# One plan for a whole two-branch kernel, and its FFT convolution cut into five blocks of 128 channels

## The chip, the cores and the metric

The kernel runs on one core of one Trainium2 chip. The metric is the time of one execution on the device in microseconds (us), the median of several runs. TensorE is called PE here (PEld is its loading of weights), VectorE DVE, ScalarE ACT, GpSimd POOL; SP is the engine that only starts DMAs, POOL starts some too.

## The reference, cut to what matters

Two branches share the rows of one input `x` (2048 x 640) and are mixed by a gate. Branch A is attention with 32 heads of 20 channels, over 8 keys at a distance of 2. Branch B is a long convolution of each of the 640 channels with a kernel K that is a sum over 192 complex modes.

```python
g = _sigmoid((x * gate_w).sum(-1, keepdims=True))
a = _A_ref(x, A_wqkv, A_wo)
b = _B_ref(x, B_A_re, B_A_im, B_B_re, B_B_im, B_C_re, B_C_im, B_log_dt, B_Dskip)
return g * a + (1 - g) * b
# in _B_ref:
P = jnp.exp(logdA[:, :, None] * l[None, None, :])
K = jnp.einsum("dn,dnl,dn->dl", Cc, P, dB).real
...
Yf = Uf * Kf[None, :, :, :]
y = irfft(Yf)[:L] + u * Dskip
```

The convolution is done with transforms of 4096 points. The kernel splits 4096 into 32 x 64, so a transform is two steps of matmuls with constants, and the way back is two more.

## The kernel before, in words

**Order of work.** `Plan.add` records tasks: a name, the engines that may run it, a duration for planning, a function that writes the instructions, what it depends on, and buffers taken and given back. The order of the tasks, and whether ACT (`A`) or DVE (`D`) runs a task that may go to either, is a list of numbers computed beforehand (`ORDER`, L48). `Plan.emit` (L137) writes the tasks in that order and chains the instructions of each engine, so each engine, SP and POOL included, works strictly in the list's order. There are two plans. "main" holds the parameters, attention, the generation of K and the convolution's first step. "tail" holds the rest of the convolution (`fft_conv`, L919). It begins after main is closed, with PSUM pools of its own.

**Attention** (branch A): transposes of x (`turn`, L191), projections (`late`, L272, evicted as `lev` into `prj` or `pv` and stored to DRAM), then eight chunks of 256 positions: five products q*k on DVE (L319) summed over heads on PE (`lg`, L325), softmax, five weighings of v on DVE (`pv`, L385, two steps of two channels and one of one), sums over the window on PE (`gat`, L390), evicted as `oT`, the output projection (`wo`, L407), evicted as `ga` and stored to DRAM by SP (`gaS`).

**Generation of K** (`KGen.plan`): ten groups of 64 channels. In each PE makes arguments (`arg`, L711), ACT takes sines (L723) and exponentials (L725), DVE makes three products (`pq`, three instructions, L743 to L745), PE sums over modes with 256 small matmuls (`kmm`, L761), and `fin` (L1147) copies the sum into `E`. After each five groups `KExpand` spreads E to X on DVE (L806), stores it to DRAM (`Kx`, L832 to L835) and loads it back as `kc` (L840) with time on partitions.

**Convolution.** First step (`f1`, `fk` for K, `fu` for the input, L1163): 160 matmuls of 128x256 with a constant, in which real and imaginary parts are columns; 40 evictions of 128x1024 into bufA (K) and big (input). The second step, in tail, runs over eight slices of frequencies: real part and imaginary part of K and of u are made separately, each by two accumulated matmuls with blocks of a constant PHI (L954, 256 matmuls of 320 columns) and evicted by ACT (32 of 128x1280). DVE makes the complex product with four multiplies (`ta`, `tc`, L979) and two additions (L982) a slice. PHI is loaded slice by slice by POOL. The inverse of the second step (L1009) is 320 matmuls on half of the rows, evicted as `cp` (20 of 128x1024) into bufA as C. The last step (`yp`, L1033) is 512 matmuls on 32x32 tiles in six groups; ACT (L1041) and DVE (L1044, L1048) gate, add `gaF`, which is the attention's result read back from DRAM, and SP and POOL store the output (L1057). Loads of gaF (L972) and of the constant psi (L969) are started by SP after POOL copies that pace them.

**PSUM** is cut into pools: main has `ar` (two buffers of two banks, for `turn`, `arg`, the first step), `tb` (two of one), `kb` and `lg` (one each). tail has two buffers of four banks, then four of two, then two of four again.

Of the kernel before, what the change touches and what calls it, by code (L numbers as in the profile page):

```python
# [36 lines left out]
def _attn_consts():  # L37
# [47 lines left out]
), "tail": (  # L85
# [66 lines left out]

class Attn:
# [22 lines left out]
    def window(self, pl, cst, pa):  # L176
# [7 lines left out]
        for n in range(2 * NKT):  # L184
            hf, kt = divmod(n, NKT)
            b = {}

            def turn(_, hf=hf, kt=kt, b=b):
                tx = b["tx"] = pa.tile([128, 2, 512], F32, name="ar")
                for i in range(8):  # L190
                    nc.tensor.matmul(tx[:, i // 4, (i % 4) * 128:(i % 4) * 128 + 128], self.xn[:, 8 * hf + i, kt * 128:(kt + 1) * 128], self.ident[:], start=True, stop=True)  # L191

            def ev(en, hf=hf, kt=kt, b=b):
                evict(nc, en, self.xT[:, hf, kt, :], b["tx"][:].rearrange("p a b -> p (a b)"))
            m = pl.add(f"turn{n}", "P", 0.447, turn, acq=["ar"], eq=1024, rdy=(14.6, 24.0)[hf])
            self.xts.append((m, pl.add(f"tev{n}", "AD", {"A": 0.905, "D": 1.133}, ev, deps=[m], rel=[("ar", m)])))

    def plan_gate(self, pl, cst, pa, g_sb, late):
# [3 lines left out]
        def logit(_):  # L202
            b["gz"] = gz = pa.tile([128, 2, 512], F32, name="ar")
# [47 lines left out]
    def plan_late(self, pl, wk, pvb, ps):  # L251
        nc = self.nc
        self.stored, mms, n, st = {}, [], 0, {}
        prjw = pvb[:, 0:15 * SC].rearrange("p (w e s) -> p w e s", w=3, e=5)
# [3 lines left out]
        for sc in range(NSC):  # L258
            c0 = sc * SC
            for which, dstS, off in ((0, self.qS, 0), (1, self.kS, HALO), (2, self.vS, HALO)):  # L260
                tag, at_ = ("prj", {}) if sc else ("prjw", {})
                evs = []
                for e in range(5):
                    b = {}

                    def mm(_, b=b, which=which, e=e, c0=c0, sc=sc):
                        if sc and "all" not in st:
                            open_(0)
                        b["pp"] = ps.tile([128, 2, 256], F32, name="tb", bufs=2)
# [21 lines left out]
    def plan_core(self, pl, pvb, g_sb, ps):  # L291
# [7 lines left out]
        lastwo = lastlg = lastpr = lastpv = None  # L299
        spreads = []  # L300
        self.npv = 0
        for sc in range(S // C):
# [4 lines left out]
            def load(nm, src, n, w, c0=c0, b=b):  # L307
# [3 lines left out]
                return pl.add(f"{nm}{c0}", "G", 0.87, fn, deps=dep(w), acq=[nm], dma=1.4)  # L311
# [4 lines left out]
            for e in range(5):  # L316
# [4 lines left out]
                def logits(_, e=e, b=b):  # L321
                    if e == 0:
                        b["lg"] = ps.tile([128, W, 64], F32, name="lg")
# [39 lines left out]
            def spread(_, sc=sc, b=b):  # L363
                b["asb"] = wk.tile([128, TB, W * 64], BF16, name="asb")
# [7 lines left out]
            asb = pl.add(f"asb{sc}", "S", 0.55, spread, deps=[st], acq=["asb"], dma=1.6)  # L372
            spreads.append(asb)
            evs = []
            for e in range(0, 5, 2):
                n = min(2, 5 - e)

                def weigh(_, e=e, n=n, b=b):
                    vt = b["vc"]
                    b["pv", e] = pvb[:, 16 * C * (self.npv % 2):16 * C * (self.npv % 2) + 16 * C].rearrange("p (w n c) -> p w n c", w=W, n=2)  # L380
                    self.npv += 1
                    aw = b["asb"][:].rearrange("p b (w t) -> p w b t", t=64)
                    for k in range(n):
                        for_e = bass.AP(vt[:].tensor, vt[:, e + k, :].offset, [list(vt[:].ap[0]), [DIL, W], [64, TB], [1, 64]])
# [52 lines left out]

NST = 192
NTR, NEX = 5, 6
NXT = 10240  # L440
PSTEPS = 26
MAGIC = 12582912.0
U16 = 65536.0 / (2.0 * np.pi)
# [798 lines left out]
```

## Time and profile before

| | us |
|---|---|
| median of 3 runs | 371.55 |
| the runs | 369.85, 373.75, 371.55 |
| the profiled execution, its time | 373.87 |
| its span, first to last instruction | 371.9 |
| busy: PE, DVE, ACT, POOL | 309.6, 308.6, 306.5, 88.0 |
| last product of the generation ends | 250.7 |
| `yp` starts | 346.7 |

How to read the lines below. A line of a group gives the source line, engine, operation, output and inputs by the program's names, partitions x elements, the count, then the busy time of the group in us, the mean duration of one in ns, and the idle time of the engine just before these instructions with what ended it. A line of the timeline gives start and length in us, then the same names, the count of merged instructions, and in brackets the idle time before. A line of a stretch gives its ends and length, and each engine's busy time with the number of instructions; PEclk is the granted clock of PE, 1 being full. A line of a DMA gives what is copied, the issuing queue, the count, the size and the median time from issue to landing. Busy time of an engine counts overlapping instructions once, so sums of durations come out some per cent above it. Durations of matmuls contain their way through the array: the pitch of a row of matmuls is seen only over many.

### The profile page before, as it was taken

How to read it: one execution, taken by the hardware profiler on the slowest of the kernel's cores; microseconds unless marked ns; L12 is line 12 of the kernel's file. 1: busy time of each engine (PE TensorE's matmuls, PEld its weight loads, DVE VectorE, ACT ScalarE, POOL GpSimd, SP SyncE). 2: the span in 40 equal slices, each digit the busy share in tenths (PEclk: the TensorE clock that was granted, in tenths of full speed). 3: DMA queues.
4: the chain of work that ended last, by engine and by line, in shares of the span. 5: the costliest groups of instructions: out<-in, count | busy, mean ns of one | idle time of the engine just before them, and what ended most of it. 6: DMA issues, size and time to landing. Idle time of an engine off the chain costs nothing. (4 is left out here: it accounts for less than half of the span.)

```text
span 371.9 us, 12255 instructions
## 1 busy us (share of the span) xinstructions
PE 309.6 (83%) x5322; PEld 185.4 (50%) x5350; DVE 308.6 (83%) x417; ACT 306.5 (82%) x413; POOL 88.0 (24%) x125
## 2 busy tenths in 40 slices
PE   0269999999999999998879999998998999979440
PEld 0135654435444645545444555566776556548330
DVE  3788997769989999999997999997785299989552
ACT  1498986599879998999999999889778699979441
POOL 8930040025002002321224225520100021210132
PEclk9999999999999999999989999999999899999855
DMA  8982287667433123881649556632640465420154
GB/s 271 370 237 55 70 239 200 198 190 243 151 108 111 39 108 101 236 260 39 178 98 317 138 184 150 197 130 74 214 142 35 104 176 146 115 51 23 38 131 120
DMA packets 38408, 55.66 MB, mean 150 GB/s; under 512 B 23620, under 2 KB 30340, under 8 KB 37844
## 3 DMA queue, kind: packets, MB, share of 16 engines
q0 software_dynamic: 7920, 28.74, 25.6%
q1 hardware_dynamic: 28980, 25.64, 24.1%
q8 instruction: 41, 0.67, 0.7%
q10 hardware_dynamic: 1456, 0.52, 0.5%
q14 instruction: 11, 0.09, 0.1%
HBM read 35.12 MB, written 19.77 MB: 148 GB/s over the span
## 5 line engine op out<-in xcount | busy, mean ns | idle before, releaser
L272 PE MATMUL tb<-bufA 128*128 128x512 bf16 x282 | 72.1, 389 | 5.5 <-ACT bufA L433 2.3
L723 ACT ACTIVATE big<-ar 128x608 bf16<-128x608 int16 x96 | 59.4, 687 | 3.3 <-PE ar L711 2.8
L711 PE MATMUL ar<-Rarg,L 64*128 64x304 bf16 (+1 forms) x480 | 53.0, 278 | 8.2 <-ACT big L723 3.0
L725 ACT ACTIVATE big<-ar 128x864 bf16<-128x864 f32 x60 | 49.6, 919 | 2.7 <-PE ar L711 2.5
L272 PEld LDWEIGHTS <-bufA 128*128 128x128 bf16 x300 | 33.1, 120 | 34.5 <-issue 12.0
L319 DVE TENSOR_TENSOR prod<-qc,kc 128x2048 bf16<-128x2048 bf16 x40 | 47.7, 1220 | 1.8 <-PE lg L325 1.7
L385 DVE TENSOR_TENSOR pv<-vc,asb 128x2048 bf16<-128x2048 bf16 x40 | 47.1, 1220 | 0.8 <-PE tb L390 0.6
L390 PE MATMUL tb<-pv,ident 128*128 128x512 bf16 (+1 forms) x182 | 37.6, 344 | 0.8 <-issue 0.5
L711 PEld LDWEIGHTS <-L 64*128 64x128 bf16 x480 | 21.7, 94 | 31.3 <-issue 26.0
L761 PEld LDWEIGHTS <-pt 128*32 128x32 bf16 (+1 forms) x2560 | 25.0, 92 | 22.9 <-issue 13.3
L761 PE MATMUL kps<-qq,pt 128*32 128x22 bf16 (+1 forms) x2560 | 35.3, 173 | 0.7 <-issue 0.7
L954 PEld LDWEIGHTS <-PHI 128*128 128x128 bf16 x256 | 25.5, 100 | 18.5 <-issue 8.4
L407 PE MATMUL tb<-wo_sb,oT 128*128 128x320 bf16 x160 | 26.8, 300 | 1.0 <-DVE ga L418 1.0
L390 PEld LDWEIGHTS <-ident 128*128 128x128 bf16 x192 | 17.7, 98 | 15.0 <-issue 1.5
L954 PE MATMUL fp<-big,PHI 128*128 128x320 bf16 x128 | 20.8, 307 | 2.6 <-ACT bufA L433 1.1
L433 ACT ACTIVATE sp_u<-fp 128x1280 bf16<-128x1280 f32 x16 | 19.7, 1236 | 3.8 <-PE fp L954 2.7
L954 PE MATMUL fp<-bufA,PHI 128*128 128x320 bf16 x128 | 20.5, 306 | 0.9 <-ACT sp_k L433 0.4
L745 DVE TENSOR_TENSOR qq<-big 128x1408 bf16<-128x1408 bf16 x24 | 21.3, 887 | 0.0
L433 ACT ACTIVATE sp_k<-fp 128x1280 bf16<-128x1280 f32 x16 | 19.7, 1237 | 1.6 <-PE fp L954 1.3
L191 PE MATMUL ar<-ident,xn 128*128 128x128 bf16 x80 | 7.8, 264 | 15.0 <-DMA xn<-in_A_x_dram 13.6
L433 ACT ACTIVATE big<-bp 128x1024 bf16<-128x1024 f32 x18 | 17.8, 1030 | 3.0 <-PE bp L1163 2.4
L433 ACT ACTIVATE prj<-tb 128x512 bf16<-128x512 f32 x27 | 16.1, 598 | 5.0 <-PE tb L272 4.7
(170 smaller groups left out, 573.8 us busy)
## 6 DMA issues: line engine op xcount, KB each, us to landing
asb<-aS SPq DMA_DIRECT2D x8, 512.0 KB, 3.9
PHI<-c_phi POOLq DMA_DIRECT2D x8, 384.0 KB, 4.6
Sprm<-pc SPq DMA_DIRECT2D x12, 240.0 KB, 3.2
L<-Sprm SPq DMA_DIRECT2D x80, 36.0 KB, 2.8
kc<-kS POOLq DMA_DIRECT2D x8, 337.5 KB, 6.0
vc<-vS POOLq DMA_DIRECT2D x8, 337.5 KB, 4.6
xn<-in_A_x_dram SPq DMA_DIRECT2D x4, 640.0 KB, 12.0
qc<-qS POOLq DMA_DIRECT2D x8, 320.0 KB, 5.8
```

Of the source, the lines that this page charges most:

```text
L272: nc.tensor.matmul(ppf, self.wq[:, kt, which * D + e:(which + 1) * D:5], self.xT[:, c0 // 1024, kt, c0 % 1024:c0 % 1024 + SC], start=(kt = ...
L319: nc.vector.tensor_tensor(b[e][:], b["qc"][:, e, :].unsqueeze(1).to_broadcast([128, W, C]), win(b["kc"][:, e, :], 0, W, DIL, C), ALU.mult)
L385: nc.vector.tensor_tensor(b["pv", e][:, :, k, :].rearrange("p w (b t) -> p w b t", t=64), for_e, aw, ALU.mult)
L390: nc.tensor.matmul(b["op", e][:, 0:n, :], ident[:], b["pv", e][:, w, 0:n, :], start=(w == 0), stop=(w == W - 1))
L407: nc.tensor.matmul(apf[:, :320], b["oT"][:, e, i * 128:(i + 1) * 128], wo_sb[:, e, hf * 320:(hf + 1) * 320], start=(e == 0), stop=(e == 4))
L433: nc.scalar.activation(o, i, ACT.Identity)
L711: nc.tensor.matmul(ar[:, g2, a0:a0 + ncol], L[rows, sb, gp, l0:l0 + 128], R[rows, c0:c0 + ncol], start=True, stop=True, tile_position=(64 ...
L723: nc.scalar.activation(dst[:, 2 * gp:2 * gp + 2, sub, :], ar[:].bitcast(I16)[:, :, 0:2 * SW:2], ACT.Sin, scale=SCL)
L725: nc.scalar.activation(dst[:, 2 * gp:2 * gp + 2].rearrange("p g s n -> p g (s n)"), ar[:, :, 0:2 * EW], ACT.Exp)
L745: nc.vector.tensor_tensor(qq[:], trg[:, :, KI:].rearrange("p a (v m) -> p a v m", v=2), exq[:, :, KI:].unsqueeze(2).to_broadcast([128, 32, ...
L761: nc.tensor.matmul(kps[32 * g:32 * g + 32, h, NM * ql:NM * ql + NM], pt[rows, k, v, :], qq[rows, k, v, :], start=(g not in started), stop= ...
L954: nc.tensor.matmul(fp[:, fl, 0:320].rearrange("p (c x) -> p c x", x=32), phis[fb][:, fl, kind, :], B[:, :, 2 * f1 + ri].rearrange("p c q g ...
```

## The change

1. There is one plan, "main"; "tail" is gone. PSUM is one tile of eight banks, from which tasks take fixed places (`Banks`), and some places overlap: a task of the convolution with place `xr` waits for the last tasks of the generation and of the softmax that use these banks (`fin9`, `at7`), one with `yr` for attention's last ones (`ga711`).
2. The generation's ten groups are now taken in five blocks of two (`HC` is 2), in an order of channels given by `PLACE`. After each block comes expansion, store and load of a fifth of K, and that block's convolution. Blocks 0 and 1 can go through while the generation runs. The first step for u of block 2 waits for block 1; the loads of K of blocks 2 to 4, and u's transforms of blocks 3 and 4, wait for the last product (their buffers lie in the generation's ring).
3. The convolution of a block stacks real and imaginary parts on the 128 partitions. The first step makes them by two matmuls with 64-wide outputs on two column halves of the array. The second step is one matmul for each of 32 frequencies instead of two for each part. u's spectrum is copied with its halves swapped by two DMAs from SBUF to SBUF (`sw`, on SP), and DVE multiplies spectrum and swapped spectrum by K's, in place (`ta`, `tb`); the additions of the complex product are made by the inverse's matmuls in PSUM, two for each output, over all 128 rows.
4. Counts: first step 640 matmuls of 64x128 (L957) for 160 of 128x256; second 320 of 128x128 (L974) for 256 of 128x320; inverse 320 of 128x128 over 128 rows (L1032) for 320 over 64; 100 evictions of 128x1024, of which the order gives 79 to ACT and 21 to DVE, for 60 of 1024 (47 and 13) and 32 of 1280 (ACT); 40 multiplies of 128x1024 (L1018, L1020) for the 32 multiplies and 16 additions (some cut in three).
5. Attention weighs one channel at a time and sums it with 40 groups of eight matmuls of 256 columns. PHI is loaded whole, once. gaF is loaded in 16 DMAs (L1202) after the last first step on u and the attention chunks that it needs; psi's halves go into a part of big. The copies that paced these are gone.
6. The last step is the same but for the order of C's channels: its operand and its output are read and written 16 channels at a time.

```diff
@@ ORDER: one list, "main", 1453 numbers; "tail" is removed
+class Banks:
+    PLACES = {"ar": (0, 2, 2), "tb": (4, 1, 2), "kb": (6, 1, 1), "lg": (7, 1, 1), "xr": (6, 2, 1), "yr": (4, 2, 1), "yp": (0, 4, 2)}
...
-HC = NCH // 2
+HC = 2
+NB = NCH // HC
+PLACE = [0, 3, 4, 1, 2]
...
+    def ring(self, name, bl, k):
+        return (("ar",), ("ar",), ("ar", "ar", "xr"), ("ar", "ar", "xr"), ("ar", "ar", "xr") if name == "u" else ("ar", "ar", "xr", "yr"))[bl][k % (4 if bl == 4 and name != "u" else 3 if bl > 1 else 1)]
...
+# first(): four groups n
+                for q in range(8):
+                    src = col(bl, 8 * n + q)
+                    for ri in range(2):
+                        nc.tensor.matmul(b["bp"][64 * ri:64 * ri + 64, q, :], src, self.F1[:, ri, :], start=True, stop=True, skip_group_check=True, tile_position=(0, 64 * ri))
+                evict(nc, en, self.S1[:, n].rearrange("p f (q g) -> p f q g", g=4), b["bp"][:].rearrange("p q (g f) -> p f q g", f=32))
+# second(): four groups k
+                for f in range(8):
+                    nc.tensor.matmul(b["sp"][:, f, :].rearrange("p (n x) -> p n x", n=4), self.Phi[:, 8 * k + f, :], self.S1[:, :, 8 * k + f, :], start=True, stop=True)
+                evict(nc, en, put(k), b["sp"][:].rearrange("p f x -> p x f"))
+# spectra_u(): first, second, then
+            for r in range(2):
+                nc.sync.dma_start(T()[1][64 * r:64 * r + 64], T()[0][64 - 64 * r:128 - 64 * r])
+# rest(): first and second for K, then for k in range(4)
+  ta:   nc.vector.tensor_tensor(T()[0][:, :, fr], T()[0][:, :, fr], slot[k], ALU.mult)   deps=[sk[k], su[k], sw]
+  tb:   nc.vector.tensor_tensor(T()[1][:, :, fr], T()[1][:, :, fr], slot[k], ALU.mult)   deps=[sk[k], sw]
+# inverse, four groups n
+                for q in range(8):
+                    for r in range(2):
+                        t = T()[r].rearrange("p (x g) f -> p x (g f)", g=4)[:, 8 * n + q]
+                        nc.tensor.matmul(b["cp"][:, q, :], t, self.GAB[:, r, :], start=(r == 0), stop=(r == 1))
+                evict(nc, en, self.C[:, PLACE[bl], :, 8 * n:8 * n + 8], b["cp"][:].rearrange("p q x -> p x q"))
...
-                        n = min(2, 5 - e)
-                        nc.tensor.matmul(b["op", e][:, 0:n, :], ident[:], b["pv", e][:, w, 0:n, :], start=(w == 0), stop=(w == W - 1))
+                        nc.tensor.matmul(b["op"][:, k, :], ident[:], b["pv", e][:, w, :], start=(w == 0), stop=(w == W - 1))
```

More of the change, by code (lines that the diff above doesn't have):

```diff
@@ L790, in shift @@
         def shift(_):
-            nc.vector.tensor_tensor(E()[:, 0, :], E()[:, 0, :], self.Dk[:, hf], ALU.add)
+            nc.vector.tensor_tensor(E()[:, 0, :], E()[:, 0, :], self.Dk[:, PLACE[bl]], ALU.add)
         def move(_):
-            nx = X["nx"] = psp.tile([128, 2, 512], F32, name="nxp", tag="ar")
-            for pt, (b0, n) in enumerate(((0, 4), (4, 3))):
-                for k in range(2):
-                    f = FIRST + b0 + k
-                    nc.tensor.matmul(nx[:, pt, 0:n * CH], S12[:, k], E()[:, f:f + n].rearrange("p m c -> p (m c)"), start=(k == 0), stop=(k == 1))
@@ new lines, in second, with mm, ev @@
+    def second(self, pl, pa, name, bl, m1, firsts, put, held, after):
+        nc, es, ms = self.nc, [], []
+        for k in range(4):
+            b, r = {}, self.ring(name, bl, k + 1)
+            def mm(_, k=k, b=b, r=r):
+                b["sp"] = pa.get(r, 128)
+                for f in range(8):
+                    nc.tensor.matmul(b["sp"][:, f, :].rearrange("p (n x) -> p n x", n=4), self.Phi[:, 8 * k + f, :], self.S1[:, :, 8 * k + f, :], start=True, stop=True)
+            def ev(en, k=k, b=b):
+                evict(nc, en, put(k), b["sp"][:].rearrange("p f x -> p x f"))
+            more = held(k)
+            if name == "k":
+                after = ms[-1:] + after
+            elif k:
+                after = ms[:1]
+            m = self.add(pl, f"s{name}{bl}{k}", 0.46, mm, r, bl, deps=firsts + self.ready, after=after, acq=[r] + more, rel=[("S1", m1)], eq=1024)
+            ms.append(m)
+            es.append(pl.add(f"s{name}e{bl}{k}", "AD", {"A": 0.905, "D": 1.13}, ev, deps=[m], rel=[(r, m)]))
+        return ms, es
@@ L1078, in gated_mix_kernel @@
     at = Attn(ctx, tc, x, A_wqkv, A_wo, gate_w, gaS, omS)
-    P, rows, gates, consts = fft_prefetch(ctx, tc, x, omS)
-    F1c = P["F1c"]
-    Bk = P["bufA"][:].rearrange("p (c f q g) -> p c f q g", c=NCH, f=64, q=8)
+    cv = Conv(ctx, tc, x, omS, gaS, out[0])
     c2 = ExitStack()
-    big = ExitStack()
+    big = ctx.enter_context(ExitStack())
     acst = c2.enter_context(tc.tile_pool(name="a2_cst", bufs=1))
@@ L1189, in gated_mix_kernel, with expand, fetch @@
-    fft_conv(tc, P, big, now["big"][:].rearrange("p (c f q g) -> p c f q g", c=NCH, f=64, q=8), gaS, o2)
+    late = at.plan_late(pl, cv.pool, pvb, ps)
+    gate = at.plan_gate(pl, acst, pa, g_sb, late)
+    at.plan_core(pl, pvb, g_sb, ps)
+    xdone = late + [gate[0]]
+    half = {}
+    def expand(bl, f):
+        shift, move, near, own, other, store = kx.expand(bl, lambda: half["E"], now, pa, kg.S12)
+        a = pl.add(f"shift{bl}", "D", 0.1, shift, deps=[f])
+        n1 = pl.add(f"move{bl}", "P", 0.25, move, deps=[f], acq=["ar"], eq=448)
+        n2 = pl.add(f"near{bl}", "AD", {"A": 0.24, "D": 0.30}, near, deps=[n1], after=half.get("x", []), rel=[("ar", n1)])
+        o1 = pl.add(f"own{bl}", "AD", {"A": 1.9, "D": 1.3}, own, deps=[a], acq=["xk"])
+        o2 = half["cp"] = pl.add(f"other{bl}", "AD", {"A": 0.85, "D": 0.45}, other, deps=[o1, n2])
+        half["x"] = [o2]
+        st = [pl.add(f"xst{bl}{e}", e, d, store, deps=[o2], dma=w, rel=[("xk", o1)]) for e, d, w in (("S", 1.25, 1.4), ("G", 0.6, 0.5))]
+        def fetch(e, bl=bl):
+            if (bl, "kc") not in half:
+                o = (None, None, 2048, 0, 20480)[bl]
+                half[bl, "kc"] = now["kk"].tile([128, 64, CH], BF16, name="kc", tag="xkc") if bl < 2 else now["big"][:, o:o + 2048].rearrange("p (t c) -> p t c", c=CH)
+            for g in (0, 1) if e == "S" else (2, 3):
+                kx.load(bl, half[bl, "kc"], g, nc.sync if e == "S" else nc.gpsimd)
+        ld = half[bl, "ld"] = []
+        for e, d in (("S", 1.4), ("G", 1.1)):
+            ld.append(pl.add(f"xld{bl}{e}", e, d, fetch, deps=st, after=list(ld), acq=["xk"] if bl < 2 and e == "S" else [], dma=0.7))
@@ new lines, in fin, with fn @@
+    def fin(c, b, m, m0, fins):
+        bl, cl = c // HC, c % HC
+        def fn(en):
+            if cl == 0:
+                half["E"] = now["kk"].tile([128, NM, CH], BF16, name="E")
+            evict(nc, en, half["E"][:].rearrange("p m (c x) -> p c m x", c=2)[:, :, :, CQ * cl:CQ * cl + CQ],
+                  b["kps"][:, :, 0:CQ * NM].rearrange("p c (q m) -> p c m q", m=NM))
+        f = pl.add(f"fin{c}", "AD", {"A": 0.38, "D": 0.433}, fn, deps=[m] + ([half["cp"]] if cl == 0 and c else []), after=fins[-1:], rel=[("kb", m0)])
+        if cl == HC - 1:
+            expand(bl, f)
+            convolve(bl)
+        return f
@@ new lines, in gated_mix_kernel @@
+    cst = pl.add("consts", "G", 1.1, cv.consts, dma=0.6)
+    phi = pl.add("phi", "G", 0.55, lambda _: nc.gpsimd.dma_start(cv.Phi[:], cv.host["phi"]), after=[cst], dma=3.2)
+    cv.ready = [cst, phi]
+    ub = []
+    for n in range(8):
+        ub.append(pl.add(f"rows{n}", "G", 1.4 if n else 0.7, lambda _, n=n: cv.rows(n), deps=ub[-1:], after=list(at.stored.values()), dma=1.65))
+    gates = [pl.add(f"gates{g}", "G", 0.55, lambda _, g=g: cv.gates(g), after=ub + [gate[1]], dma=0.1) for g in range(4)]
@@ new lines, in gated_mix_kernel, with convolve @@
+    om = pl.add("om32", "D", 0.1, lambda _: nc.vector.tensor_copy(cv.om32[:], cv.omF[:]), deps=gates)
+    cps = []
+    def convolve(bl):
+        cv.pqs = list(kg.pqs)
+        cv.spectra_u(pl, pa, bl, ub, xdone + params)
+        firsts, cp = cv.rest(pl, pa, bl, lambda: half[bl, "kc"], half[bl, "ld"])
+        cps.extend(cp)
+        if bl < 2:
+            for f in firsts:
+                f.rel.append(("xk", half[bl, "ld"][0]))
+    cv.big = lambda: now["big"]
+    kg.plan(pl, pa, pk, params, opened, fin)
@@ new lines, in gated_mix_kernel, with gated @@
+    psi = lambda: now["big"][:, 0:4096].rearrange("p (u r x) -> p u r x", r=2, x=32)
+    psis = [pl.add(f"psi{h}", "S", 0.5, lambda _, h=h: nc.sync.dma_start(psi()[:, 32 * h:32 * h + 32], cv.host["psi"][:, 32 * h:32 * h + 32]), after=kg.pqs, dma=1.6) for h in range(2)]
+    def gated(n):
+        if n == 0:
+            cv.gaF = cv.pool.tile([128, 16, D], BF16, name="gaF", tag="uga")
+        for j in range(4):
+            nc.sync.dma_start(cv.gaF[32 * j + 8 * n:32 * j + 8 * n + 8], cv.gaS[j][8 * n:8 * n + 8])
@@ new lines, in gated_mix_kernel @@
+    gas = []
+    for n in range(4):
+        gas.append(pl.add(f"gaF{n}", "S", 1.6, lambda _, n=n: gated(n), deps=at.gated[2 * n:2 * n + 2], after=cv.lastu + gas[:1], dma=2.0))
+    by = {t.name: t for t in pl.tasks}
+    for t, r, bl in cv.lazy:
+        t.deps += [by[n] for n in {"xr": ("fin9", "at7"), "yr": ("ga711", "lev59")}.get(r, ())]
+        if bl > 2 and t.name[:2] in ("fu", "su"):
+            t.deps.append(kg.pqs[-1])
+    for bl in (2, 3, 4):
+        for t in half[bl, "ld"]:
+            t.deps.append(kg.pqs[-1])
@@ L1192 @@
+    for h in range(2):
+        psis[h].deps += [by[f"fk{3 - h}{n}"] for n in range(4)]
+    cv.last(ctx, pl, pa, cps, gas + [om], psi, psis, c2.close)
+    pl.emit(tc)
 @with_exitstack
```

558 lines of the change are left out of this document (234 added, 324 removed), and 88 rows, old and new, of the table ORDER.

## The prediction, made before the changed kernel was run

> **What bounds the kernel now.** I read the page's first two parts, then the busy time by stretch, then the groups of instructions with shapes kept apart, then single stretches in order of time, then the DMA issues.
>
> ```profile
> PE 309.6 (83%) x5322; PEld 185.4 (50%) x5350; DVE 308.6 (83%) x417; ACT 306.5 (82%) x413; POOL 88.0 (24%) x125
> ```
>
> No engine is the bound of the whole: three stand at 82 to 83%, so the share says nothing until the span is cut where the work changes.
>
> ```profile
> core 0: us, PE busy (x) PEld busy (x) DVE busy (x) ACT busy (x) POOL busy (x), PEclk, DMA share, GB/s
> 0.00:100.00 100.00, 76.95 (x685) 41.27 (x695) 80.20 (x99) 74.95 (x101) 34.73 (x49) 1.00 0.68 206
> 100.00:250.70 150.70, 140.53 (x3193) 78.01 (x3206) 143.83 (x200) 142.28 (x219) 38.03 (x46) 0.99 0.51 148
> 250.70:346.70 96.00, 85.31 (x946) 60.98 (x946) 74.61 (x105) 81.90 (x84) 9.32 (x18) 0.98 0.36 105
> 346.70:371.90 25.20, 6.85 (x512) 5.18 (x512) 9.96 (x16) 7.39 (x10) 5.94 (x12) 0.57 0.40 107
> ```
>
> 250.7 is where DVE ends the last product of the kernel generation, 346.7 where the last step (`yp`) starts. From 100 to 250.7 DVE and ACT are 95.4% and 94.4% busy: full. In the 96 us behind that ACT is 85.3% and DVE 77.7% busy, 81.5% on the mean: here lie 14 us of idle ACT and 21 of idle DVE. Of this stretch, 300 to 340 alone is fuller (DVE 18.93 and 18.45, ACT 18.61 and 17.42 in its two halves of 20 us, 91.8%); the hollow is 250 to 300, attention's end and the passage from one plan to the other.
>
> ```profile
> 290.85 1.24 ACT L433 ACTIVATE sp_u<-fp 128x1280 bf16<-128x1280 f32 x1 [2.30 <-PE fp L954]
> 295.04 0.82 DVE L979 TENSOR_TENSOR ta<-sp_u,sp_k 128x1280 bf16<-128x1280 bf16 x1 [6.92 <-ACT sp_u L433]
> ...
> L433 ACT ACTIVATE sp_u<-fp 128x1280 bf16<-128x1280 f32 x16 | 19.7, 1236 | 3.8 <-PE fp L954 2.7
> L433 ACT ACTIVATE sp_k<-fp 128x1280 bf16<-128x1280 f32 x16 | 19.7, 1237 | 1.6 <-PE fp L954 1.3
> L433 ACT ACTIVATE big<-bp 128x1024 bf16<-128x1024 f32 x18 | 17.8, 1030 | 3.0 <-PE bp L1163 2.4 <-DVE qq L745 0.6
> ...
> L435 DVE CAST bufA<-cp 128x1024 bf16<-128x1024 f32 x8 | 9.3, 1219 | 0.0
> ...
> L979 DVE TENSOR_TENSOR ta<-sp_u,sp_k 128x1280 bf16<-128x1280 bf16 x16 | 12.7, 820 | 8.2 <-ACT sp_u L433 6.9 <-ACT sp_k L433 1.3
> L982 DVE TENSOR_TENSOR Y<-ta,tc 128x1280 bf16<-128x1280 bf16 x14 | 11.6, 826 | 0.5
> L743 DVE TENSOR_TENSOR pt<-big 128x1024 bf16<-128x1024 bf16 x24 | 16.5, 687 | 0.5 <-issue 0.3 <-ACT big L723 0.2
> ```
>
> The first two lines are the seam: ACT 2.30 us and DVE 6.92 us with nothing to do. The others are my prices (busy time of the group, then mean ns of one).
>
> **Work removed and added.** ACT loses 32 evictions of 1280 (19.7 + 19.7), 35 of the first step (17.8 and its sister's 17.0) and 12 of the inverse (a group of 11.4): 85.9. It gains 79 of 1024 at 0.99 (17.8/18): 78.2, so -7.7; nine fewer of 512 from the projections and attention (-5.4) are paid back by three small kinds that come over from DVE (E, X, a transpose: +5.2 with oT). ACT: -7.9. DVE loses ta, tc and Y (40.4 with their small forms) and gains 40 multiplies of 128x1024 at 0.687, 27.5: -12.9. But it makes 21 of the 100 evictions, at 1.22 (25.6), where it made 13 (15.4): +10.2; and five, two and two more of 512 (at 0.69, +6.2, against six fewer of E, 3.1 less) and copies of X in 52 pieces for 22 (small ones have 0.17 to 0.2 each; +4.7), less 1.2 of the rest. DVE: +3.9. Both together -4.0, times 0.96 since neighbours overlap (in the third stretch DVE's rows make 77.6, its busy time 74.6), -3.8: under 2 us an engine. The additions in PSUM that the stacking saves are paid back by where the evictions go.
>
> PE, by pitch: 16 matmuls of 128 columns with a new weight each take 1.06 us and 8 take 0.61, so 0.056 each; the half-array inverse takes 2.20 for 72, 0.031.
>
> ```profile
> 29.36 0.61 PE L191 MATMUL ar<-ident,xn 128*128 128x128 bf16 x8
> ...
> 38.37 1.06 PE L191 MATMUL ar<-ident,xn 128*128 128x128 bf16 x16
> ...
> 334.35 2.20 PE L1009 MATMUL cp<-GAB,Y 64*128 64x128 bf16 x72 [0.26 <-DVE Y L982]
> ...
> 84.48 0.40 PE L325 MATMUL lg<-prod,ind 128*32 128x512 bf16 x4
> ```
>
> Out go 160 at 0.11, 256 at 0.136, 320 at 0.031: 62. In come 640 halves of 64 columns' width and 640 full ones at 0.056 (36). No row has a half-width stationary; four quarter-width ones (last line) take 0.40 where one takes 0.39, so they run side by side: I take 0.031, the sum is 56; the other end is 0.056 with no overlap at all (72), or 0.15 where a load of 94 ns is also bare (132).
>
> [...]
>
> **Where the work lies.** Stretches 2 and 3 hold 218.4 us DVE and 224.2 ACT; less 3.8 they are 438.8. Behind the last product the changed order leaves on ACT 52 evictions (51.0), 13 of attention, a table load and three small (10.5), on DVE 20 evictions (24.4), 32 multiplies (22.0), 9 weighings at 1.19 (10.7) and 4.5 of the rest: 61.5 and 61.6, times 0.96 59.3 each. Before it is 74.6 against 81.9. So the third stretch shrinks and is balanced, and the second takes (438.8 - 118.6)/2 = 160.1 an engine. At the 94.9% it has now, that is 168.7 us, for 150.7. Bounds: 96% (166.8) and 92% (174.0), as swaps and one more round trip hang on the same two PSUM buffers (`ar`).
>
> Third stretch: at the 91.8% of 300 to 340, 64.6 us; ends 94.9% (62.5) and today's 81.5% (72.8). I take 91.8% since attention's last two chunks now fill the gaps, as in 100 to 250.
>
> **Moved and added DMAs.** Five swaps of 2 x 512 KB on SP, five stores and loads of K for two, each smaller; 16 loads of gaF for 8; POOL loses the five late PHI loads and ten pacing copies and stores and loads a fifth of K five times, off the path. Prices: `asb` 512 KB 3.9 us to landing, gaF 5.0, Kx 3.0 to 6.0 (gaS and today's Kx).
>
> ```profile
> asb<-aS SPq DMA_DIRECT2D x8, 512.0 KB, 3.9
> ...
> gaS<-ga SPq DMA_DIRECT2D x8, 320.0 KB, 3.0
> ...
> gaF<-gaS SPq DMA_DIRECT2D x8, 320.0 KB, 5.0
> ...
> Kx<-X SPq DMA_DIRECT2D x2, 640.0 KB, 6.0
> ```
>
> One place stands out. SP runs, in order, gaF0, the store of the fifth block's K, its load (which waits for that store), gaS6, then the swap of block 3. From block 4's first step on u, which releases gaF0: 1.4 + 1.0 issue, 3.0 to 6.0 landing, 0.8 + 0.4 + 0.7 issue, 3.9 to 6.0 landing: 11.2 to 16.3 us. DVE reaches block 3's first multiply after five evictions, one weighing and two multiplies: 8.7. So DVE waits 2.5 to 7.6, ACT with it (two buffers of spectra). PE's own lateness covers a part; I take 4 (ends 0 and 7.6). The end's loads are hidden: behind attention's last eviction gaS7, gaF3 and half of psi take 9.5 to 9.8 us, beside 14 evictions on ACT, 13.7; each us beyond is paid whole.
>
> Blocks 2 to 4 use PSUM banks of the generation and of attention too. The matmul that takes one waits for their last reader (`fin9`, `at7`, `ga711`), and PE's whole queue behind it; the order puts it after them, by one eviction at the closest: none taken, ends 0 and 1.
>
> Last step: 25.2, the same instructions. Its matmuls read 16 elements at a stretch for 160; nothing in the trace reads so short, none to +3 (what PE has of the chain).
>
> **Sum.** 100.0 (first stretch; ACT's work ahead of the first sine is 53.4 by rows for 56.1, no gain taken) + 168.7 + 68.6 (64.6 + 4) + 25.2 = 362.5 span. The profiled execution took 373.87 for 371.9, so 1.97 around it: 364.5. It stands 2.3 above the median 371.55 of the three runs; 362.2, say 362.
>
> **Rivals.**
> Tighter: the second stretch at 96%, the third at 94.9%, no wait on SP: 166.8 + 62.5 for 237.3, 354; with the first sine 3 us earlier 351. For it: conv work gives both engines something at every gap of the generation. Against: 94.9% was never passed for long.
> Sparse chain: the third stretch at today's 81.5% with the 7.6 wait: 72.8 + 7.6 for 68.6, 374; without that wait 366. For it: each block is a chain of four PE steps with an eviction between each. The change then does not do what it says.
> PE the bound (the slower side): stretch 3 asks PE for 320 + 224 full matmuls (30.4), 384 halves (11.7), attention's 80 at 0.11 and 45 at 0.136 (14.9) and about 1.5 of generation: 58.5, as much as DVE and ACT. At 0.056 a half it is 68.3, the stretch 74.4 + 4, time 372: no change. From there on it decides; at 0.08 it is 77.5, 84.4 + 4, 382; at 0.15 (every load bare) 104.4, 113.7 + 4, 411.
> Multiply at one element a cycle: its operands come in runs of 8. If it takes the 1.16 of the f32 tensor_tensor (128x960) for 0.687, DVE has 15 us more in stretch 3 (32 x 0.47): 59.3 + 14.5, 80.4 + 4, 378. Against: Y writes runs of 4 at 0.826 for 1280, no dearer than ta.
>
> **Chances.** Forecast, 354 to 368: 0.54. Tighter: 0.15. Sparse: 0.14. PE: 0.11, of it 0.02 for bare loads. Multiply: 0.06. A measurement of this kernel tells about 1% from no change, 3.7 us. Faster: 0.15, nearly all of 0.54 and a little of the sparse one: 0.69; same 0.14; slower 0.17. The range 347 to 378 leaves out 2 in 10 at most, most of it PE; the likeliest one's own is 354 to 368.
>
> **What would show it.** The last product near 269 and the last step's start near 337; DVE and ACT alike, near 90%, between them; the halves' 16 matmuls in about 0.65 us; a multiply at 0.69; DVE idle 2 to 8 us ahead of block 3's multiplies, by the swap. Wrong it is if PE waits for nothing there while DVE and ACT wait for PE, or if the second stretch falls under 92%.

## The result and the profile after

The changed kernel takes 411.53 us at the median (410.82 to 414.7, four runs), the kernel before 372.51 in the same comparison (369.85 to 373.75): 1.1075 times, 95% interval 1.0987 to 1.1162. It is slower by 39 us; 362 was forecast. The profiled execution took 411.71 for a span of 409.8.

The page's first part of the changed kernel, and the line of its second part for the DMA engines (tenths of busy time in 40 slices) with what they moved:

```profile
PE 326.2 (80%) x6024; PEld 222.3 (54%) x6024; DVE 307.1 (75%) x443; ACT 299.7 (73%) x416; POOL 80.9 (20%) x117
...
DMA  8925773377421628747475447252311579865354
GB/s 276 399 73 162 215 198 114 130 186 228 149 84 35 186 72 287 237 152 195 114 202 146 135 119 211 88 152 99 86 33 22 78 191 94 111 97 75 56 133 130
```

DVE has 1.5 us less work than before and ACT 6.8 (forecast: 3.9 more and 7.9 less); PE has 16.6 more. Slower by 39 us, with less work on the two engines that were full: the time came in idle. Slices 33 to 36 (from 328 us on) read 7, 9, 8, 6 in DMA with 191, 94, 111 and 97 GB/s under them, where slice 2 reads 9 with 399: the transfers were busy and moved little.

Busy time by stretch, cut at the end of the last product (270.2) and at the last step's start (387.7):

```profile
core 0: us, PE busy (x) PEld busy (x) DVE busy (x) ACT busy (x) POOL busy (x), PEclk, DMA share, GB/s
0.00:100.00 100.00, 75.98 (x696) 39.47 (x700) 81.22 (x102) 76.39 (x102) 34.38 (x49) 0.97 0.65 201
100.00:270.20 170.20, 164.76 (x3616) 106.91 (x3615) 158.24 (x250) 156.20 (x235) 38.82 (x53) 1.00 0.53 151
270.20:387.70 117.50, 78.34 (x1218) 70.79 (x1215) 58.16 (x75) 59.75 (x71) 1.74 (x3) 0.85 0.51 88
387.70:409.80 22.10, 7.07 (x504) 5.15 (x504) 9.50 (x16) 7.40 (x10) 5.96 (x12) 0.50 0.44 122
```

The whole loss is in the third stretch: 117.5 us for 68.6, with DVE at 58.2 and ACT at 59.8 us of work (59.3 each forecast), so half of it idle. What ended the idle time there, from the timeline (in brackets the idle time before the instruction and what ended it):

```profile
334.98 0.53 ACT L439 ACTIVATE ga<-banks,g_sb 128x320 bf16<-128x320 f32 x1 [8.90 <-DMA gaS<-ga]
340.44 0.69 DVE L1018 TENSOR_TENSOR big<-big,spare 128x1024 bf16<-128x1024 bf16 x1 [14.62 <-DMA big<-big]
360.50 0.69 DVE L1018 TENSOR_TENSOR big<-big,spare 128x1024 bf16<-128x1024 bf16 x1 [9.01 <-DMA big<-big]
387.75 1.84 PE L1059 MATMUL banks<-bufA,big 32*32 32x160 bf16 x152 [14.35 <-DMA big<-c_psi]
```

Four waits, 46.9 us on three engines (ACT's and the first of DVE's run side by side), and all four are for DMAs that SP issued: a store of `ga` (its buffer is wanted again), the swaps of blocks 3 and 4, and the second half of `psi`. SP's own timeline (start, time in issue, what) shows what they stood behind:

```profile
315.47 1.31 SPq L1202 DMA_DIRECT2D gaF<-gaS  x4
316.88 0.38 SPq L854 DMA_DIRECT2D Kx<-X  x1
317.36 0.65 SPq L855 DMA_DIRECT2D Kx<-X  x1
329.22 1.47 SPq L859 DMA_DIRECT2D big<-Kx  x2
330.80 0.39 SPq L450 DMA_DIRECT2D gaS<-ga  x1
331.29 1.16 SPq L999 DMA_DIRECT2D big<-big  x2
332.50 5.18 SPq L1202 DMA_DIRECT2D gaF<-gaS  x4
337.79 1.11 SPq L999 DMA_DIRECT2D big<-big  x2
339.06 1.76 SPq L1196 DMA_DIRECT2D big<-c_psi  x1
340.87 12.15 SPq L1202 DMA_DIRECT2D gaF<-gaS  x4
356.06 0.38 SPq L450 DMA_DIRECT2D gaS<-ga  x1
373.40 1.28 SPq L1202 DMA_DIRECT2D gaF<-gaS  x4
374.79 0.35 SPq L1196 DMA_DIRECT2D big<-c_psi  x1
```

The order is the one the prediction read; the times are not. The store of K, its two parts issued at 316.88 and 317.36, has landed only when its load starts at 329.22, for 3 to 6 us in the prediction; the swap issued at 337.79 is waited for until 360.5. The chain of waits that ended last has the same transfers (start, time):

```profile
317.36 11.72 DMA Kx<-X
...
337.37 18.63 DMA gaF<-gaS
356.06 17.32 DMA gaS<-ga
...
374.79 12.91 DMA big<-c_psi
```

The last store of `ga` takes 17.3 us, for the 3.0 that a store of `ga` took before. In front of each stands a batch of four `gaF` loads. In the trace's DMA records a `gaF` load is 8 packets of 20480 bytes, one to a partition; the 128 of them took 3.01 us each at the median, 6.8 GB/s, 369 us together. The eight packets of a load run side by side, and the four loads of a batch follow each other (a batch of 10.8 us from 360.7 to 371.5). In the kernel before the packets of `gaF` had 10240 bytes, 32 to a DMA, and took 0.615 us, 16.7 GB/s.

PE's side: 64 half-width matmuls of the first step take 3.88 us, 0.060 each, where the prediction took 0.031.

```profile
302.37 1.06 PE L974 MATMUL banks<-spare,PHI 128*128 128x128 bf16 x16
304.19 3.88 PE L957 MATMUL banks<-F1c,Usb 128*64 128x128 bf16 x64 [0.76 <-ACT spare L456]
```

### The profile page after: what moved, and what is told of

Read it like the earlier page. It is cut to its first block, busy times and chain, and to the rows that moved or that the text cites. A ratio compares the mean times of both kernels' runs of the same rounds, so it can differ in the third digit from the quotient of the medians.

```text
span 409.8 us, 13703 instructions
## 1 busy us (share of the span) xinstructions
PE 326.2 (80%) x6024; PEld 222.3 (54%) x6024; DVE 307.1 (75%) x443; ACT 299.7 (73%) x416; POOL 80.9 (20%) x117
## 4 chain that ended last, share of the span: by engine, by line
PE 45%; ACT 24%; DMA 18%; issue 4%; DVE 4%; SPq 3%; POOL 0%; POOLq 0%; DVEq 0%; ACTq 0%
PE banks L291 10%; PE banks L957 8%; ACT big L750 7%; PE banks L736 6%; PE banks L410 6%; ACT big L748 5%; DMA gaF<-gaS 5%; DMA gaS<-ga 4%; PE banks L430 4%; PE banks L785 4%; DMA big<-c_psi 3%; DMA xn<-in_A_x_dram 3%; DMA Kx<-X 3%; ACT bufA L456 3%; PE banks L974 2%
## 5 line engine op out<-in xcount | busy, mean ns | idle before, releaser
L291 PE MATMUL banks<-bufA 128*128 128x512 bf16 x300 | 75.2, 392 | 5.1 <-DVE bufA L458 3.1
L748 ACT ACTIVATE big<-banks 128x608 bf16<-128x608 int16 x120 | 73.6, 687 | 4.7 <-PE banks L736 3.7
L456 ACT ACTIVATE spare<-banks 128x1024 bf16<-128x1024 f32 x47 | 47.2, 1023 | 29.5 <-PE banks L957 13.9
L736 PE MATMUL banks<-Rarg,L 64*128 64x304 bf16 (+1 forms) x480 | 51.2, 277 | 5.6 <-ACT big L748 3.1
L750 ACT ACTIVATE big<-banks 128x864 bf16<-128x864 f32 x60 | 49.8, 904 | 4.5 <-PE banks L736 4.3
L404 DVE TENSOR_TENSOR pv<-vc,pv 128x2048 bf16<-128x2048 bf16 x40 | 48.2, 1218 | 6.1 <-PE banks L410 4.6
L410 PE MATMUL banks<-pv,ident 128*128 128x256 bf16 x320 | 40.9, 273 | 1.9 <-issue 1.9
L456 ACT ACTIVATE bufA<-banks 128x1024 bf16<-128x1024 f32 x37 | 36.2, 1028 | 7.9 <-PE banks L1032 5.6
L785 PE MATMUL banks<-qq,pt 128*32 128x22 bf16 (+1 forms) x2560 | 36.0, 173 | 0.0
L430 PE MATMUL banks<-wo_sb,oT 128*128 128x320 bf16 x160 | 27.8, 311 | 7.8 <-ACT ga L439 7.8
L974 PE MATMUL banks<-spare,PHI 128*128 128x128 bf16 x320 | 23.1, 221 | 1.5 <-ACT bufA L456 0.5
L1018 DVE TENSOR_TENSOR big<-big,spare 128x1024 bf16<-128x1024 bf16 x8 | 5.5, 688 | 23.7 <-DMA big<-big 23.6
```

Of the source, the lines that this page charges most:

```text
L291: nc.tensor.matmul(ppf, self.wq[:, kt, which * D + e:(which + 1) * D:5], self.xT[:, c0 // 1024, kt, c0 % 1024:c0 % 1024 + SC], start=(kt = ...
L404: nc.vector.tensor_tensor(b["pv", e][:].rearrange("p w (b t) -> p w b t", t=64), for_e, aw, ALU.mult)
L410: nc.tensor.matmul(b["op"][:, k, :], ident[:], b["pv", e][:, w, :], start=(w == 0), stop=(w == W - 1))
L430: nc.tensor.matmul(apf[:, :320], b["oT"][:, e, i * 128:(i + 1) * 128], wo_sb[:, e, hf * 320:(hf + 1) * 320], start=(e == 0), stop=(e == 4))
L456: nc.scalar.activation(o, i, ACT.Identity)
L736: nc.tensor.matmul(ar[:, g2, a0:a0 + ncol], L[rows, sb, gp, l0:l0 + 128], R[rows, c0:c0 + ncol], start=True, stop=True, tile_position=(64 ...
```

## The experiments

Theories at the start. A: a load of 8 rows uses few DMA engines. B: pieces of 20 KB are slow by their length. C: the first step's pitch sets the end. Behind them, as a rival to all, SP's queue by itself. Executions of kernels that are alike up to there differ by up to 7 us in when the last product starts (268.5 to 275.6), so besides the time I give the distance from the last product's start to where the last step's matmuls run on (their first eight may stand earlier): 118.5 us in the changed kernel (269.27 to 387.75), 69.5 forecast (68.6 from that product's end, and 0.9 for the product). Most kernels below were run once. The distance repeats better than the time: it is 78.2 and 78.3 in the two profiled executions of one kernel (e8, e12).

**e1: two steps' rows in one load, at the later one's place.**

```diff
-        for j in range(4):
-            nc.sync.dma_start(cv.gaF[32 * j + 8 * n:32 * j + 8 * n + 8], cv.gaS[j][8 * n:8 * n + 8])
+        for j in range(4 * (n % 2)):
+            nc.sync.dma_start(cv.gaF[32 * j + 8 * n - 8:32 * j + 8 * n + 8], cv.gaS[j][8 * n - 8:8 * n + 8])
```

> The loads of gaF come in 8 DMAs of 16 partitions x 20 KB in place of 16 of 8 partitions x 20 KB: two steps' worth together, at the place of the later step. Changed kernel: 411.5 us. Theory A (few engines: a DMA of 8 rows occupies 8 of the 16 DMA engines, and the trace's 128 packets of 20480 bytes took 3.01 us at the median, 369 us of engine time, 46 us on each of 8 engines but 23 on each of 16): the end comes 15 to 25 us sooner, 387 to 397. Theory B (long pieces: a packet of 20480 bytes is slow by its length, whichever engine takes it): the packets stay near 3 us and the time falls by under 10 us. Theory C (the first step's half-width matmuls, 0.060 us in place of 0.031, set the end): 411, no change.

Measured: 382.42 us, distance 89.3. More than A asked for, and the packets still take 2.72 us each, as B has it. The run changes two things at once, the number of rows and the place on SP; e11 changes the place alone.

**e2: the same loads cut in two, packets of 10 KB.**

```diff
-            nc.sync.dma_start(cv.gaF[32 * j + 8 * n:32 * j + 8 * n + 8], cv.gaS[j][8 * n:8 * n + 8])
+            for v in (0, 8):
+                nc.sync.dma_start(cv.gaF[32 * j + 8 * n:32 * j + 8 * n + 8, v:v + 8], cv.gaS[j][8 * n:8 * n + 8, v:v + 8])
```

> Each load of gaF is cut in two along the positions: 32 DMAs of 8 partitions x 10 KB. The kernel before moved the same bytes in packets of 10240 bytes that took 0.615 us at the median. Theory A (few engines): the same 8 engines carry the same bytes, so 405 to 415. Theory B (long pieces): packets of 10240 bytes near 0.6 to 1.0 us, the batches land in 4 to 6 us in place of 12 to 18, and the time is 370 to 385. Theory C: 411.

Measured: 415.21 us, distance 117.7; packets of 10240 bytes take 1.50 us, again 6.8 GB/s. B falls: the length of a piece does not matter, the rate per packet stays.

**e3: nearly nothing loaded.**

```diff
-            nc.sync.dma_start(cv.gaF[32 * j + 8 * n:32 * j + 8 * n + 8], cv.gaS[j][8 * n:8 * n + 8])
+            nc.sync.dma_start(cv.gaF[32 * j + 8 * n:32 * j + 8 * n + 8, 0:1], cv.gaS[j][8 * n:8 * n + 8, 0:1])
```

> Leaves out 15 of 16 positions of each gaF load (each partition loads its first position's 1280 bytes, and the last step reads that one for all 16), so the output is not the reference's; the same 16 DMAs, the same waits and places on SP's queue. Theories A and B (the gaF transfers are what the end waits for, through the rings behind them): last step starts near 340 in place of 387.8, time 362 to 372. Theory C, or SP's order by itself (a wait on the queue whatever is moved): 400 to 411.

Measured: 382.49 us, distance 84.7. The bytes of `gaF` cost 34 us of the distance and C is not the cause of those; but the time stays above the 362 to 372 of A and B, so 15 us lie elsewhere.

**e4: the loads issued by POOL.** In `gated`, `nc.sync` becomes `nc.gpsimd`, and the task's engine "G".

> The 16 gaF loads as they are, issued from POOL's queue in place of SP's, with the same place in the order. If what costs is that SP's other transfers (Kx, the swaps, the store of ga, psi) stand behind them in the same rings: those land in 3 to 6 us again, and the time falls to 375 to 390. If the DMA engines themselves are what is full (theories A and B): under 10 us gained, 402 to 412. Theory C: 411.

Measured: 412.21 us, distance 116.4, packets of 20480 bytes 2.41 us. From 340 to 360 the DMA share is 0.96 at 126 GB/s. Another queue does not help here: the transfers themselves are still slow. SP's queue has no `gaF` load in it now, and still the swap of block 3, which SP issues from 334.2 on, is there for DVE only at 366.6; POOL's `gaF` loads run from 336.4 to 367.2:

```profile
366.60 0.69 DVE L1018 TENSOR_TENSOR big<-big,spare 128x1024 bf16<-128x1024 bf16 x1 [37.96 <-DMA big<-big]
```

So the slow loads hold up what another queue carries too. The run does not clear the order, though: the first `gaF` load, on POOL from 318.7, now stands ahead of the part of K's store that POOL issues (320.8), and K's load waits for that.

**e5: the same 16 loads of 8 rows, on every fourth partition.**

```diff
-            nc.sync.dma_start(cv.gaF[32 * j + 8 * n:32 * j + 8 * n + 8], cv.gaS[j][8 * n:8 * n + 8])
+            nc.sync.dma_start(cv.gaF[32 * j + n:32 * j + 32:4], cv.gaS[j][8 * n:8 * n + 8])
+    psis = psis[..., [8 * (i % 4) + i // 4 for i in range(32)]]
```

(The gates' load and the output's rows follow the same permutation.)

> The changed kernel with its 16 gaF loads as they are in number, size (8 rows of 20 KB) and order, but row n*8+a of each 32 goes to partition 4a+n in place of 8n+a, so that a load writes every fourth partition of 32 and not 8 neighbours (psi's columns, the gates and the output's rows are permuted to match). Theory A (a DMA of 8 rows occupies 8 engines, and those are the limit): the packets of 20480 bytes keep their 3.0 us and the time its 411. Theory D (8 neighbouring partitions are written through a narrow path, near 54 GB/s a DMA as 8 packets at 6.8 GB/s show, whatever engines carry it): the packets take 0.8 to 1.5 us, the batches land in 4 to 6 us, and the time comes to that without most of the load, 380 to 386.

Measured: 384.25 us, distance 92.1; the packets of 20480 bytes take 1.03 us at the median, 161 us together for 369. Number, size, order and queue of the loads are as in the changed kernel, so A falls, which would have kept 3.0 us, and D stands: where the rows land decides. 26.4 us of the distance are this. The rates: 8 packets at 6.8 GB/s are 54 GB/s into 8 neighbouring partitions, 16 at 7.5 (e1) 120 into 16 neighbours, and 8 at 20.0 160 into the same number of rows spread over 32. The medians of the last two mix packets; the steadiest give 109 (e1, second and fourth load of each batch, 3.0 us a packet) and 215 (e5, third batch, 0.76 us a packet, 26.9 GB/s). What it is that neighbouring partitions share, no run shows; these rates are what was measured.

**e6: on top of e5, weights from neighbouring elements.**

```diff
-        col = lambda bl, s: self.Usb[:, :, 80 * (s // 16) + 16 * PLACE[bl] + s % 16]
+        col = lambda bl, s: self.Usb[:, s, 0:64]
...
-        fs = self.first(pl, pa, "k", bl, lambda bl, s: kc()[:, :, s], ld + self.ready, self.us, ms)
+        fs = self.first(pl, pa, "k", bl, lambda bl, s: kc()[:, 2 * s:2 * s + 2, :], ld + self.ready, self.us, ms)
```

> On top of the permuted rows: the first step's 64-column weights are read from 64 neighbouring elements of x's rows and of the kernel's expansion in place of 64 elements 320 bytes (64 bytes for the expansion) apart, so it transforms other numbers than the reference does; number, size and order of the matmuls stay. Theory C1 (the pitch of 0.060 us per half is the strided weight load, 204 ns against 98 ns for 128 neighbouring columns): the pitch falls to 0.031 to 0.040, PE has 13 to 18 us less work, and the last step starts 6 to 15 us sooner than without this. Theory C2 (two halves of a pair do not overlap one another's load, whatever the stride): the pitch stays 0.056 to 0.062 and the time within 2 us.

Measured: 372.46 us, distance 83.5 for 92.1, and the last product 3.4 us sooner (265.4; 265.8 in e9, while all the kernels with strided weights lie between 268.5 and 275.6). The group of x's weight loads in e5, then in e6 (busy time, mean ns of one; L957 is L958 here, as these kernels have a line more):

```profile
L958 PEld LDWEIGHTS <-Usb 128*64 128x64 bf16 x320 | 19.3, 205 | 1.6 <-issue 1.2
```

```profile
L958 PEld LDWEIGHTS <-Usb 128*64 128x64 bf16 x320 | 10.4, 109 | 3.1 <-issue 2.2
```

The halves that use them, in e5's timeline, then in e6's:

```profile
311.07 3.85 PE L958 MATMUL banks<-F1c,Usb 128*64 128x128 bf16 x64
```

```profile
302.93 1.08 PE L958 MATMUL banks<-F1c,Usb 128*64 128x128 bf16 x32
```

32 halves in 1.08 us, 0.034 each: C1. The halves' pitch comes from the strided weight load: with neighbouring weights it is near the 0.031 that the prediction took. The expansion's weights, 64 bytes apart, load in the same 204 to 205 ns as x's at 320 bytes.

**e7: both halves of psi at the first one's place, on top of e5.** The first task loads both, the second none.

> On top of the permuted rows: both halves of psi are loaded at the place of the first, and none behind the last gaF load. If the last step waits for psi's second half behind the gaF rings: it starts 4 to 14 us sooner than with the permuted rows alone, 368 to 378. If PE's chain sets the start of the last step by itself (as where the gaF loads were left out, 358): within 2 us of the permuted rows.

Measured: 388.51 us, distance 90.9 for 92.1: nothing. The last step's matmuls then wait for an eviction (`bufA`, 1.13 us) and not for `psi`; the chain that ended last runs through a swap, the last store of `ga` and the last `gaF` load. What ended last in the changed kernel was not the only thing that was late.

**e11: on top of e5, the first four loads issued with the next four**, so that nothing of `gaF` waits at the head of SP's queue.

```diff
+        for m in {0: (), 2: (0, 2)}.get(n, (n,)):
+            for j in range(4):
+                nc.sync.dma_start(cv.gaF[32 * j + m:32 * j + 32:4], cv.gaS[j][8 * m:8 * m + 8])
```

> The permuted rows with 16 loads of gaF, the first four of them issued at the place of the next four, so that nothing on SP waits for block 4's first step on u ahead of the fifth block's store of K, the store of ga and the swap of block 3. Measured from the last product to the last step, where single executions compare best: 92.1 us with the permuted rows alone, 78.2 with the pairs. If what the pairs took away is the wait of the first gaF load at the head of SP's queue: 78 to 83 us. If it is the number of DMAs (each waits for the one eight before it on SP, and sixteen loads push the others back by two rounds of eight): 88 to 93 us.

(Eight before: in the trace SP's DMAs of this stretch take eight semaphores in turn, numbers 107, 109 to 114 and 117, and each one waits on its semaphore for the DMA that had it last.)

Measured: 374.38 us, distance 79.5 for 92.1: the first load's wait was worth 12.6 us. SP's timeline in e5, then in e11:

```profile
314.98 2.67 SPq L1203 DMA_DIRECT2D gaF<-gaS  x4
317.76 0.38 SPq L854 DMA_DIRECT2D Kx<-X  x1
...
323.55 1.36 SPq L859 DMA_DIRECT2D big<-Kx  x2
325.02 0.38 SPq L450 DMA_DIRECT2D gaS<-ga  x1
325.51 1.18 SPq L1000 DMA_DIRECT2D big<-big  x2
```

```profile
301.32 0.36 SPq L854 DMA_DIRECT2D Kx<-X  x1
...
304.58 1.47 SPq L859 DMA_DIRECT2D big<-Kx  x2
306.16 0.37 SPq L450 DMA_DIRECT2D gaS<-ga  x1
315.23 1.17 SPq L1000 DMA_DIRECT2D big<-big  x2
317.81 6.67 SPq L1204 DMA_DIRECT2D gaF<-gaS  x8
```

In e5 the store of K starts at 317.8, 2.8 us behind the `gaF` load that waited 21.8 us for block 4's first step on u; without that load in front it starts at 301.3, when its data is ready. The swap of block 3 goes out 10 us sooner, and DVE's wait for it, 11.6 us in e5, is gone.

**e8, e12: pairs of steps on every second partition** (8 loads of 16 rows, the place of e1; psi, gates and output rows follow).

```diff
+        for j in range(4 * (n % 2)):
+            nc.sync.dma_start(cv.gaF[32 * j + n // 2:32 * j + 32:2], cv.gaS[j][8 * n - 8:8 * n + 8])
```

> Two changes to the loads of gaF together: two steps' rows in one DMA at the later step's place (8 DMAs of 16 rows), and row 16n+a on partition 2a+n, so that a DMA writes every second partition of 32. So nothing of gaF waits on SP's queue ahead of the fifth block's store of K and of the store of ga, and half as many DMAs stand between a DMA and the one eight before it on SP. If what is left after the narrow writes is SP's queue (the wait of the first gaF load on block 4's first step, 22 us in which the store of ga and the swap stand behind it, and a queue of eight outstanding DMAs): the last step starts 5 to 12 us sooner than with permuted rows alone (361), the time is 370 to 379. If PE's chain of half-width steps alone sets it (358 where nearly nothing of gaF was loaded): 380 to 384.

> The pairs of gaF loads on every second partition once more, the kernel that computes the whole and was quickest so far, in more rounds. If the narrow writes and SP's queue were all that made the change slower, and the strided weights use up what the change gains: within 1% of the kernel before, 368 to 376. If the change gains besides: under 368.

Measured: e8 377.52 us, four runs from 370.52 to 379.37, too far apart to tell; so it was run again as e12: 373.32 (12 runs) against 373.19 for the kernel before, 0.9993 times, interval 0.9952 to 1.0034. Distance in e12 78.3, against 89.3 in e1, which differs only in the partitions, and 79.5 in e11, which has twice as many loads: the number of DMAs is worth 1.2 us at most. Busy time of e12 in the same stretches:

```profile
0.00:100.00 100.00, 75.09 (x681) 39.37 (x690) 81.29 (x102) 75.76 (x101) 34.63 (x49) 0.98 0.65 201
100.00:269.70 169.70, 164.11 (x3609) 107.16 (x3618) 158.51 (x250) 156.84 (x236) 37.78 (x53) 1.00 0.54 152
269.70:347.00 77.30, 73.13 (x1209) 66.67 (x1207) 58.02 (x75) 59.27 (x71) 1.75 (x3) 1.00 0.52 134
347.00:370.00 23.00, 6.38 (x512) 4.84 (x511) 9.49 (x16) 7.40 (x10) 6.10 (x12) 0.64 0.41 117
```

Now PE is busy 73.1 of 77.3 us in the third stretch, 95%, with DVE and ACT at 75 and 77%: PE is the bound there.

**e9, e10: on top of the pairs, neighbouring weights (as e6), and psi at once (as e7).**

> The pairs of gaF loads on every second partition, and besides the first step's weights from neighbouring elements (other numbers are transformed than in the reference; number and order of the matmuls stay). With the narrow writes, SP's queue and the strided weights all gone, nothing should be left of the difference to the forecast if these three are all of it: 358 to 366, the last step's start 333 to 342. If something else costs (the swaps, the chain of the five blocks): 368 to 374.

> The pairs of gaF loads on every second partition, with both halves of psi loaded at the first one's place. If the last step waits for psi behind the last gaF loads once these are quick: 3 to 6 us below the pairs alone. If it waits for the last gaF loads or for the inverse's evictions: within 2 us.

Measured: e9 362.82 us, distance 72.5. Three removals bring the time to the forecast, in one execution, with other numbers in the first step as in e6. e10 377.75, distance 78.5: `psi` is again worth nothing.

## Why the prediction was wrong

Point by point, in its own order.

- The second stretch: right in time, by luck. The last product starts at 269.27, "near 269", and ends at 270.2 for 268.7, though with 157 us of work an engine for 160 and 92.4% for 94.9%: two misses that cancel.
- The work of the third stretch: right, 58.2 and 59.8 for 59.3. The multiply: 0.69 us as taken (0.683 to 0.688 at the median), so that rival is out.
- The failed step is "The end's loads are hidden", and the price under it, "gaF 5.0". The 5.0 was read from loads of 32 partitions x 10 KB and carried to loads of 8 x 20 KB. With the changed shape a packet has 6.8 GB/s for 16.7, and the slow loads hold up what is in flight beside them: K's store 11.7 us for 3 to 6, a swap 22 for 3.9 to 6.0 (6.1 from its first issue to its last packet in e12, 312.38 to 318.48), the last store of `ga` 17.3 for 3.0. Shown by e5: 26.4 us. The prediction counted the loads (16 for 8) and not their rows.
- SP's order: the place was named right ("One place stands out") and priced wrong. DVE's wait at block 3's first multiply was 14.6 us for the 4 taken, 7.6 at the outer end; still 11.6 with the spread rows. What it missed is that everything on SP behind the first `gaF` load waits with it, the store of `ga` too, whose buffer ACT then waits for (8.9 us). Shown by e11: 12.6 us.
- The halves' pitch: 0.060 for the 0.031 taken; the end "0.056 with no overlap at all" was near the true size, and for another reason than overlap. The prediction priced the halves from rows with neighbouring weights. The old first step's pitch of 0.11 could not have warned it: those matmuls move 256 columns, and attention's, which move 256 with neighbouring weights, have 0.11 too. The weight loads of the kernel before could have, strided (`Usb`, `kc`) and neighbouring (`ident`):

```profile
L1163 PEld LDWEIGHTS <-Usb 128*128 128x128 bf16 x80 | 9.8, 162 | 1.5 <-issue 0.7
L1163 PEld LDWEIGHTS <-kc 128*128 128x128 bf16 x80 | 9.2, 145 | 2.4 <-issue 1.5
L390 PEld LDWEIGHTS <-ident 128*128 128x128 bf16 x192 | 17.7, 98 | 15.0 <-issue 1.5
```

The size, 205 ns for 64 columns, stands in no row of before. Shown by e6: 8.6 us in the third stretch (5.8 from e12 to e9). The last product is 3.4 us sooner besides (3.0 from e12 to e9), but single executions differ by more than that.

- The 0.15 end, where every load is bare, did not come: in the changed kernel the halves follow each other by 0.060 us with loads of 204 to 206 ns each, in e6 by 0.034 with loads of 109. That the kernel takes the 411 us of that end is chance: PE is busy 78.3 us in the third stretch for the 104.4 that the rival asks.
- The last step: 22.1 us in the changed kernel and 23.0 in e12 for 25.2; the reads of 16 elements cost nothing.
- Slips in the working that move the forecast by under 0.5 us: the evictions that ACT loses add up to 85.6 and not 85.9, and 0.96 times 61.5 and 61.6 is 59.0 and 59.1. The rival on the multiply took the 1.16 of 960 elements for 1024; 1.24 would make it 381 in place of 378.

From the distance of 118.5 the spread rows take 26.4, the order on SP 12.6, fewer loads 1.2, neighbouring weights 5.8: 72.5, against 69.5. The shares hold for this order of removal: behind e1's pairs, which clear SP's queue first, the spread rows are worth 11.0 (89.3 to 78.3), and the pairs themselves 29.2. The 3.0 us left are open; in e9's time they are balanced by the last product, which ends 2.0 us ahead of 268.7, and a last step 2.9 shorter than forecast. That e9 meets the forecast is in part luck. The rival that came nearest, once the DMAs were mended, is "PE the bound" at 0.056 a half, 372: e12 has 373.3. So in e12 what the change gains elsewhere is used up by the strided weights, which the new first step loads twice: the third stretch's 384 halves at 0.060 are 23 of PE's 73 us there. A version that computes the whole with neighbouring weights was not tried.

## What to carry to other kernels

Price a DMA by the partitions that it writes, and not by its bytes and number alone: here a load of 8 rows had 54 GB/s into 8 neighbouring partitions and 160 into 8 spread over 32. A load that is cut to start sooner can lose more by landing on few neighbouring partitions than it gains (26.4 us here), and it slowed what was in flight beside it (the last store of `ga` took 17.3 us for 3.0). Before a load goes to a shared queue, list what stands behind it and ask when its own wait ends; a load whose data and buffer are not both free belongs behind those that are (12.6 us here). A matmul's pitch is not to be read from rows with neighbouring weights where its own are strided (0.060 us for 0.034 here): look first at what the weight loads of the two kinds take.

## What was not expected of the hardware

- The `gaF` loads into 8 neighbouring partitions ran at 54 GB/s (8 packets at 6.8) with packets of 20480 bytes (the changed kernel) and of 10240 (e2) alike, from SP's queue; into 8 rows on every fourth partition, packets of 20480 bytes had 20.0 GB/s each at the median and 26.9 at their quickest (0.76 us, e5).
- 64 weight columns at a stride of 64 or of 320 bytes took 204 to 206 ns to load in the changed kernel, with a pitch of 0.060 us; 64 neighbouring ones took 109 ns (x, e6), and the matmuls followed by 0.034. In the kernel before, 128 columns of x 160 bytes apart took 162 ns, less than 64 here; why is open.
- A swap, two DMAs of 512 KB within SBUF with 8192 bytes a packet, runs for 4.9 us from its first packet to its last where no `gaF` load is ahead of it (block 3's in e12, 313.55 to 318.48). Beside other DMAs it was waited for 10 us (issued by 326.7, multiply at 336.94 in e5), and beside slow `gaF` loads 22.
